# Gated attention with a ReGLU block on one core: raw scores for a second query tile in both halves of six heads, other tile counts per round, last stage reordered

## The chip, the core and the metric

The kernel runs on one NeuronCore of a Trainium2 chip. The core has a matrix engine (TensorE, PE in the profile; its weight loads, which overlap the matmuls, are PEld) and four others: VectorE (DVE), ScalarE (ACT), GpSimd (POOL) and SyncE (SP), which here only issues DMAs. Each engine works through its own list of instructions in order; semaphores join the lists. TensorE writes into eight PSUM banks of 128 x 512 floats, which are called bank 0 to bank 7 here. The metric is the device time of one execution in microseconds; lower is better.

## What is computed

```python
def _A_ref(x, wqkv, wo):          # S = 2048 tokens, D = 448, H = 16 heads of Dh = 28
    qkv = transpose((x @ wqkv).reshape(B, S, 3, H, Dh), 2, 0, 3, 1, 4)
    q, k, v = qkv[0], qkv[1], qkv[2]
    p = softmax(einsum("bhqd,bhkd->bhqk", q, k) * Dh ** -0.5)
    o = einsum("bhqk,bhkd->bhqd", p, v)
    return transpose(o, 0, 2, 1, 3).reshape(B, S, D) @ wo

def _B_ref(x, W_gate, W_up, W_down):                                    # F = 1792
    gate, up = x @ W_gate, x @ W_up
    return (gate * (gate > 0) * up) @ W_down

g = sigmoid((x * gate_w).sum(-1, keepdims=True))
return g * _A_ref(x, wqkv, wo) + (1 - g) * _B_ref(x, W_gate, W_up, W_down)
```

Everything is in float32. Matmuls run on operands that are split into a high and a low part, so each product is a sum of several matmuls.

## The kernel before, in words

**Stages.** First the projections: Q, K and V of all heads are computed and written to DRAM. Then 32 rounds, two for each head: round r belongs to head h = r // 2 and handles 8 of its 16 key tiles (128 keys each) against all 2048 queries, which are four query tiles j = 0 to 3 of 512. Last, a stage with the down projection (56 steps of 12 matmuls, four token tiles of 14 steps each), the output product of the attention, and the gated sum.

**A round.** Its matmuls stand in the order that a string of the table `ROUNDS` gives. Each letter is one instruction or a few: `s` a score matmul, whose tile ScalarE turns into exp (`scores`); `m` a score matmul whose maximum over the keys VectorE takes (`smax`), for a later head; `x` one of the matmuls of a gate/up tile (20 in a tile, in `gu_mm`); `r` a raw score matmul for the next round, copied out by ScalarE (`raw_scores`); `d` VectorE's running maximum over those copies (`raw_max`); `e` ScalarE's exponential of a raw tile of this round (`raw_exp`). A digit is the bank. Behind the string come the half-height last terms of the gate/up tiles, the rest of the exponentials, and 64 narrow matmuls of the weighted sum with V into bank 3 (`pv`).

**Two ways to the maximum.** The softmax needs the largest score of each query. For most query tiles it is found ahead of time, by `smax`: one matmul and one VectorE reduction for each 128 queries and 512 keys. For a raw tile no such pass is made: the scores of the round are copied out as they are, VectorE keeps a running maximum, and the end of the round before (`raw_top`) reduces it over the partitions: on VectorE two transposes, a reduction, four copies, a small reduction and a small transpose; then a DMA to DRAM (`mr_d`) and a DMA that broadcasts it back to all partitions. Next, GpSimd subtracts it from each raw tile (`raw_less`, 8 tiles for one query tile, 16 for two), and ScalarE takes the exponential. `raw_js(r)` says which query tiles are raw: j = 3 in every round from 2 on, and j = 2 too in the second (odd) round of the heads in `WIDE`. The odd round's sums are brought to the even round's maximum with a factor (`factors`, a GpSimd product behind the subtractions).

**What stands behind what.** At the end of a round VectorE's list has `raw_top` for the next round, then `spill_h` for the one or two gate/up tiles of the round (the product of gate and up, which frees banks 5 and 7 and goes to DRAM), then the copy or the sum that takes the weighted sum out of bank 3. `raw_top` writes its maxima over those that this round's subtractions read, so it waits for them. GpSimd's list has the subtractions, the factor product, the DMA of the spilled tiles, and in the early rounds the low halves of gate/up weights (`split_f`), then small products for the normalisation of the head before.

**The last stage** is a list `todo` of steps, run in order; a step `(down, i)` first issues the loads for step i + 4 (`fetch_d`: 128 rows of W_down and a tile of gate*up, from SyncE) and the splits for step i + 2 (`split_d`, ScalarE then VectorE). Between them stand the split of the output weight (`split_wo`), the row sums, their broadcast and the normalisation of head 15 (`row_sums`, `spread`, `normalise`), and for each token tile the load of the attention output (`fetch_o`), its split and four output products (`wout`).

## Time and profile before

| | us |
|---|---|
| median of 3 runs | 1220.13 (1219.09 to 1220.66) |
| the profiled execution | 1217.39 |
| its span, first to last instruction | 1215.6 |
| projections, up to the end of round 0's weighted sum | 168.5 |
| rounds 1 to 31 | 168.5 to 1025.6 |
| last stage | 1025.6 to 1215.6 |
| TensorE busy | 1205.0 |
| VectorE, ScalarE, GpSimd busy | 904.6, 815.7, 554.4 |

In a row of a group, after the names, stand the count, the busy time and the mean length in ns, then the idle time before it and what ended it. The busy time is the union of the group's own instructions; TensorE's overlap with those of other groups, so their busy times add up to more than the engine's. In a row in order of time the first two numbers are the start and the length in us. `PEclk` in the rows of a stretch is the granted clock, the third number from the end.

### The profile page before, as it was taken

Reading aid. Unit: us, or ns where it says so; the run is one execution under the profiler, and the core shown is the slowest. Engines: PE = TensorE matmul, PEld = TensorE weight load, DVE = VectorE, ACT = ScalarE, POOL = GpSimd, SP = SyncE. Lnnn points to the kernel's source line nnn. Section 1 sums busy time; section 2 is a strip of 40 time slices with the busy share of each in tenths; the row PEclk is TensorE's granted clock in tenths of the full one; section 3 lists DMA queues with packets and bytes.
Section 4 is the critical chain, followed back from the end, with each engine's and each line's share of the span. In section 5 each row is a group of like instructions: output and inputs, shape, how many; then the busy total and the mean of one; then the engine's idle time right before and its main releaser. Section 6 shows DMA issues by size and latency. Waiting matters only on the chain.

```text
span 1215.6 us, 18731 instructions
## 1 busy us (share of the span) xinstructions
PE 1205.0 (99%) x6399; PEld 866.3 (71%) x6399; DVE 904.6 (74%) x1606; ACT 815.7 (67%) x1615; POOL 554.4 (46%) x561
## 2 busy tenths in 40 slices
PE   9999999999999999999999999999999999899998
PEld 6888766666666666666666666656666756789997
DVE  6498777877887897888888889988888862453342
ACT  5311667788788777887888787888788886422121
POOL 4332325566553745474548446543847654300000
PEclk9999999999999999999999999999999999899999
DMA  8956745363645454445634343554353433653432
GB/s 298 341 212 245 252 167 188 111 205 103 213 151 176 136 166 122 130 123 185 193 119 156 108 127 108 166 187 137 109 171 90 146 96 101 221 184 113 139 105 81
DMA packets 68275, 193.99 MB, mean 160 GB/s; under 512 B 14850, under 2 KB 21602, under 8 KB 63754
## 3 DMA queue, kind: packets, MB, share of 16 engines
q1 hardware_dynamic: 55188, 148.02, 38.4%
q0 software_dynamic: 12560, 44.32, 10.2%
q8 instruction: 50, 0.82, 0.3%
q10 hardware_dynamic: 432, 0.46, 0.1%
q14 instruction: 45, 0.37, 0.1%
HBM read 132.09 MB, written 61.11 MB: 159 GB/s over the span
## 4 chain that ended last, share of the span: by engine, by line
PE 92%; ACT 3%; DMA 3%; DVE 1%; issue 0%; SPq 0%; POOL 0%; ACTq 0%; DVEq 0%
PE b L690 22%; PE b L728 19%; PE b L282 13%; PE b L309 13%; PE b L985 9%; PE b L503 6%; PE b L317 5%; PE b L521 3%; PE b L944 3%; ACT P L311 2%; DMA hr<-h_d 1%; DMA or<-o_d 1%; ACT P L321 1%; DMA wor<-wo_d 1%; DMA rb<-l_d 0%
## 5 line engine op out<-in xcount | busy, mean ns | idle before, releaser
L284 DVE TENSOR_REDUCE mx<-b 128x1 f32<-128x512 f32 x736 | 478.4, 686 | 50.6 <-PE b L282 45.0
L311 ACT ACTIVATE P<-b 128x512 f32<-128x512 f32 x728 | 402.8, 625 | 58.6 <-PE b L309 55.6
L690 PE MATMUL b<-X,wg 128*128 128x512 f32 (+1 forms) x1232 | 407.5, 400 | 0.3 <-POOL wg L187 0.3
L282 PE MATMUL b<-K,Q 128*128 128x512 f32 x736 | 272.5, 392 | 0.3 <-DVE mx L284 0.3
L309 PE MATMUL b<-Q,K 128*128 128x512 f32 x736 | 270.0, 392 | 0.0
L690 PEld LDWEIGHTS b<-X,wg 128*128 128x128 f32 (+1 forms) x1232 | 218.9, 188 | 67.5 <-issue 21.2
L728 PE MATMUL b<-P,v 128*32 128x512 f32 x1696 | 226.8, 594 | 0.0
L350 POOL TENSOR_TENSOR V<-V,P 128x512 f32<-128x512 f32 x168 | 211.0, 1296 | 24.2 <-DMA P<-mr_d 24.2
L712 POOL DMA_DIRECT2D h_d<-rl x56 | 31.3, 559 | 302.4 <-DVE rl L706 295.7
L350 POOL TENSOR_TENSOR P<-P,P 128x512 f32<-128x512 f32 x120 | 150.8, 1294 | 30.6 <-DMA P<-mr_d 15.4
L324 DVE TENSOR_TENSOR P<-b,P 128x512 f32<-128x512 f32 x231 | 156.4, 684 | 9.2 <-ACT V L321 3.8
L309 PEld LDWEIGHTS b<-Q,K 128*128 128x128 f32 x736 | 138.0, 188 | 33.5 <-ACT P L311 1.2
L282 PEld LDWEIGHTS b<-K,Q 128*128 128x128 f32 x736 | 138.0, 188 | 33.5 <-ACT P L311 1.3
L728 PEld LDWEIGHTS b<-P,v 128*32 128x32 f32 x1696 | 63.3, 110 | 121.5 <-issue 111.0
L985 PE MATMUL b<-WD,hh 128*128 128x448 f32 x672 | 142.0, 372 | 4.2 <-DVE WD L184 2.7
L985 PEld LDWEIGHTS b<-WD,hh 128*128 128x128 f32 x672 | 128.2, 191 | 16.7 <-DVE WD L184 3.1
L321 ACT ACTIVATE V<-b 128x512 f32<-128x512 f32 x160 | 94.7, 611 | 41.4 <-PE b L317 39.6
L728 PE MATMUL b<-V,v 128*32 128x512 f32 x352 | 113.8, 594 | 0.4 <-ACT V L354 0.4
L317 PE MATMUL b<-Q,K 128*128 128x512 f32 x288 | 111.2, 393 | 0.0
L178 ACT ACTIVATE hh<-hr 128x512 fp32r<-128x512 f32 x56 | 35.3, 631 | 110.8 <-PE b L985 109.4
L354 ACT ACTIVATE V<-V 128x512 f32<-128x512 f32 x168 | 96.6, 674 | 0.0
L184 DVE TENSOR_TENSOR hh<-hr,hh 128x512 fp32r<-128x512 f32 x56 | 38.6, 690 | 58.7 <-ACT hh L178 58.4
(103 smaller groups left out, 1080.1 us busy)
## 6 DMA issues: line engine op xcount, KB each, us to landing
wg<-wgs_d SPq DMA_DIRECT2D x42, 896.0 KB
K<-qk_d SPq DMA_DIRECT2D x64, 224.0 KB
Q<-qk_d SPq DMA_DIRECT2D x64, 224.0 KB
h_d<-rl POOLq DMA_DIRECT2D x56, 256.0 KB, 3.7
hr<-h_d SPq DMA_DIRECT2D x56, 256.0 KB
wgs_d<-wg SPq DMA_DIRECT2D x14, 896.0 KB
qk_d<-st POOLq DMA_DIRECT2D x21, 512.0 KB, 4.7
wgr<-wgu SPq DMA_DIRECT2D x13, 512.0 KB
```

What stands on the lines that cost most here:

```text
L282: nc.tensor.matmul(ps, Q[h][:, u * P:(u + 1) * P], K[h % 3][:, c * TB:(c + 1) * TB], start=True, stop=True)
L284: nc.vector.tensor_reduce(MX[h][:, at:at + 1], ps, axis=AX.X, op=OP.max)
L309: nc.tensor.matmul(ps, K[h % 3][:, kt * P:(kt + 1) * P], Q[h][:, j * TB:(j + 1) * TB], start=True, stop=True)
L311: nc.scalar.activation(prob(i, j), ps, AF.Exp, scale=SCALE)
L317: nc.tensor.matmul(ps, K[h % 3][:, kt * P:(kt + 1) * P], Q[h][:, j * TB:(j + 1) * TB], start=True, stop=True)
L321: nc.scalar.activation(own, ps, AF.Copy)
L324: nc.vector.tensor_tensor(run(3 - j), ps, run(3 - j) if i % 8 > 1 else prob(i - 1, j), op=OP.max)
L350: nc.gpsimd.tensor_tensor(own, own, top(3 - j), op=OP.subtract)
L354: nc.scalar.activation(own, own, AF.Exp, scale=SCALE)
L690: nc.tensor.matmul(ps, WS[i][rows, s, a], xf(i // NF, b)[rows], start=(n == 0), stop=(n == NT - 1))
L728: nc.tensor.matmul(po[32 * j:32 * j + 32], VH[h][:, i % NK], prob(i, j), start=(i == i0), stop=(i == i0 + ni - 1))
L985: nc.tensor.matmul(ACC[i // NF][t][:, :D], HH[i][:, a, t * P:(t + 1) * P], WD[:, f, b], start=(f == 0 and n == 0), stop=(f == NF - 1 and n ...
```

## The change

Three things are changed.

1. A new set `BOTH` = (4, 6, 8, 10, 12, 13), and head 2 joins `WIDE`. In the heads of `BOTH` both query tiles 2 and 3 are raw in both rounds; in head 2 in the second round. For a head of `BOTH`, `smax` covers 8 blocks of 128 queries instead of 12. In the even rounds of `BOTH` the raw tiles of j = 2 lie in the buffer `V`, in the odd ones in their own slots, so that those of two successive rounds don't meet.
2. The table `ROUNDS` is replaced. Gate/up tiles per round in the cycle of four rounds that heads 5 to 12 repeat were 1 (odd head, second half), 2, 2 (a `WIDE` head) and 2 (the next head's first half); the odd head now has 1 tile in its first half and 2 in its second. The rounds still do 55 of the 56. The next weights are asked for when a round's tiles are finished (`fin`) and no longer when they are begun.
3. In the last stage the load of the output weight stands behind the first four `fetch_d`, the reciprocal of head 15's row sums before the first down step, its normalisation before the eighth (was: the fifth), the splits of the output weight before steps 4 to 7 (was: 2 and 3), the first `fetch_o` before step 8 (was: 4) and from SyncE's queue (was: GpSimd's), its products before step 13, and head 15's last writes go to SyncE's queue.

**GpSimd, round 12** (head 6, first half; `os` is the weighted sum of a head, `V` and `P_...` are raw tiles, `P_1587` and `P_1539` the maxima). Before (the first three and the last of round 12's eight):

```order
L737 DMA ls_4297<-os_4078 128x1x16
L350 TENSOR_TENSOR P_1091<-P_1091,P_1587 128x512
L350 TENSOR_TENSOR P_1133<-P_1133,P_1587 128x512
L350 TENSOR_TENSOR P_1177<-P_1177,P_1587 128x512
L350 TENSOR_TENSOR P_1378<-P_1378,P_1587 128x512
L712 DMA h_d_4521<-rl_4499 128x512
L712 DMA h_d_4524<-rl_4501 128x512
L758 TENSOR_TENSOR os_4078<-os_4078,rb_4405 128x512
L187 TENSOR_TENSOR mh_4568<-mr_4567,mh_4568 12x128
L350 TENSOR_TENSOR V<-V,P_1587 128x512 x16
L369 TENSOR_TENSOR os_4564<-os_4564,fa_4590 64x512
```

Now (the first four and the last two of the 16 of round 12, and the first two of round 13's):

```order
L741 DMA ls_4312<-os_4036 128x1x16
L354 TENSOR_TENSOR P_1091<-P_1091,P_1539 128x512
L354 TENSOR_TENSOR V<-V,P_1539 128x512
L354 TENSOR_TENSOR P_1133<-P_1133,P_1539 128x512
L354 TENSOR_TENSOR V<-V,P_1539 128x512
L354 TENSOR_TENSOR P_1378<-P_1378,P_1539 128x512
L354 TENSOR_TENSOR V<-V,P_1539 128x512
L716 DMA h_d_4532<-rl_4507 128x512
L716 DMA h_d_4535<-rl_4509 128x512
L762 TENSOR_TENSOR os_4036<-os_4036,rb_4494 128x512
L189 TENSOR_TENSOR mh_4579<-mr_4578,mh_4579 8x128
L354 TENSOR_TENSOR V<-V,P_1539 128x512
```

Eight subtractions have become 16, and 16 more follow in round 13 as before.

**TensorE, start of round 14** (`b_69` to `b_76` are banks 0 to 7; L690/L694 gate/up, L282/L286 maxima, L309/L313 scores, L317/L321 raw scores). Before:

```order
L728 MATMUL b_72<-V,v_3874 32x512 x2
L690 MATMUL b_73<-X_166,wg_1242 128x512
L309 MATMUL b_70<-Q_177,K_174 128x512
L317 MATMUL b_75<-Q_177,K_174 128x512
L282 MATMUL b_76<-K_175,Q_178 128x512
L282 MATMUL b_71<-K_175,Q_178 128x512
L690 MATMUL b_73<-X_166,wg_1242 128x512
L309 MATMUL b_69<-Q_177,K_174 128x512
```

Now:

```order
L732 MATMUL b_72<-V,v_3886 32x512
L694 MATMUL b_73<-X_166,wg_1242 128x512
L321 MATMUL b_76<-Q_177,K_174 128x512
L286 MATMUL b_69<-K_175,Q_178 128x512
L321 MATMUL b_75<-Q_177,K_174 128x512
L694 MATMUL b_73<-X_166,wg_1242 128x512
L313 MATMUL b_71<-Q_177,K_174 128x512
```

Bank 7 (`b_76`), which `spill_h` of round 13 empties, is wanted by the second matmul of the round and no longer by the fourth.

**VectorE, last stage** (`WD` and `hh` are the splits for the down steps, `rs` the reciprocal, `os` head 15's weighted sum). Before:

```order
L184 TENSOR_TENSOR hh_9174<-hr_9127,hh_9174 128x512
L184 TENSOR_TENSOR WD<-wdr_9132,WD 128x448
L184 TENSOR_TENSOR hh_9183<-hr_9134,hh_9183 128x512
L745 RECIPROCAL rs_9198<-ls_9110 128x16
L184 TENSOR_TENSOR hh_9212<-hr_9138,hh_9212 128x512
L184 TENSOR_TENSOR hh_9237<-hr_9179,hh_9237 128x512
L184 TENSOR_TENSOR hh_9262<-hr_9208,hh_9262 128x512
L758 TENSOR_TENSOR os_8952<-os_8952,rb_9201 128x512
```

Now:

```order
L186 TENSOR_TENSOR hh_9219<-hr_9172,hh_9219 128x512
L749 RECIPROCAL rs_9222<-ls_9155 128x16
L186 TENSOR_TENSOR hh_9236<-hr_9176,hh_9236 128x512
L186 TENSOR_TENSOR hh_9257<-hr_9180,hh_9257 128x512
L186 TENSOR_TENSOR hh_9278<-hr_9232,hh_9278 128x512
L186 TENSOR_TENSOR hh_9299<-hr_9253,hh_9299 128x512
L186 TENSOR_TENSOR hh_9322<-hr_9274,hh_9322 128x512
L186 TENSOR_TENSOR hh_9345<-hr_9295,hh_9345 128x512
L186 TENSOR_TENSOR hh_9368<-hr_9318,hh_9368 128x512
L762 TENSOR_TENSOR os_8997<-os_8997,rb_9225 128x512
```

Between the reciprocal and the product that uses it stood three splits of `hh`, and now seven (the splits of `WD` in between are left out here).

The diff, cut to its core:

```diff
 ROUNDS = [
...
-    ("xs0xm1r7m6m2r3dxs0s1xs6m7xs2xm3s1m0s7xm6r3s2m1xs0xds6m7s1s2m0r3xm6s1xs2s0dm7m6xs1m3r2r7xds0xs6dxes1xxm3m2xr0"
-     "s7s6xedm3r1m2xs7s0ds6"),
-    ("xr6s2xm7xr1m6r3m0dxr2s1xs6xr7dxm0s1xs2s3dxxm0s6m1s2m3s7xs6m0m1s2m7s3s6r0xr2xm3xs6r7dxxs3xdxs0m6s1xxr3r2xs1xs"
-     "0dxddxr7m3s1xds0xm2s3r1xm7xr2m0dxs3xxexdexm0r3xxm1xdxer2xxr1dxs0d"),
...
+    ("xxs2s6m0s1r3m7xr2xm6m1r7s3xdm0r2xm6s1s3xr7xr0ddm1xs6s3xs2xxs6xds3m7m2r0xr1dxs3xds6r2m7xds3exs0xm6xm7r1r2m3xr"
+     "0xxedr7xxxexddr1xxr2dm0m3exxxxxdeexdexr0xexm1xs2xd"),
+    ("xxs0r2m7xm3r1s6m0ds7xs2m3xm6xr0xs1s2s7ds3m6xxxm0m1xs6xm7xs2m3s0m1em7xm6s3es2xm1xxr7m0xm6em2xxer3ds0xxxem1xdx"
+     "s0m2xxm7xr0xm3dem1xer2xxxr3exxdxs1dm0xxxm2xm1"),
...
-WIDE = (4, 6, 8, 10, 12, 13)
+WIDE = (2, 4, 6, 8, 10, 12, 13)
+
+BOTH = (4, 6, 8, 10, 12, 13)
...
-        return [] if r < 2 else [3, 2] if r % 2 and r // 2 in WIDE else [3]
+        return [] if r < 2 else [3, 2] if r // 2 in (WIDE if r % 2 else BOTH) else [3]
...
-            if r % 2 == 0:
+            if j == 3 and r % 2 == 0:
                 return slot(k)[:, 3]
+            if j == 2 and r % 2 and r // 2 in BOTH:
+                return slot(k)[:, 2]
...
-        return NK if h == 0 else NK - 4
+        return NK if h == 0 else NK - 8 if h in BOTH else NK - 4
...
-            side(h).dma_start(o_d[DH * h:DH * (h + 1), j * TB:(j + 1) * TB], o[32 * j:32 * j + DH])
+            nc.sync.dma_start(o_d[DH * h:DH * (h + 1), j * TB:(j + 1) * TB], o[32 * j:32 * j + DH])
...
-        if asked < NB * NF and parts == 2 * NF and (asked == NF or nxt >= asked - 2):
+        if asked < NB * NF and parts == 2 * NF and (asked == NF or fin >= asked - 2):
...
-        queue = nc.sync if tb else nc.gpsimd
-        queue.dma_start(r[:, 0:3], o_d[0:3 * P, t].rearrange("(c p) t -> p c t", p=P))
+        nc.sync.dma_start(r[:, 0:3], o_d[0:3 * P, t].rearrange("(c p) t -> p c t", p=P))
...
-    todo = [(gate_up, i) for i in range(done, NB * NF)]
+    todo = [(split_d, 0)] + [(gate_up, i) for i in range(done, NB * NF)] + [(split_d, 1), (row_sums, H - 1), (spread, H - 1)]
...
-    before(1, (row_sums, H - 1), (spread, H - 1))
-    before(4, (normalise, H - 1))
+    before(7, (normalise, H - 1))
     for c in range(4):
-        before(2 + c // 2, (split_wo, c))
-    for tb, load, split, at in ((0, 4, (9, 10), (12, 12, 13, 13)), (1, 8, (12, 14), (17, 18, 19, 20)), (2, 21, (23, 25), (28,) * 4),
+        before(4 + c, (split_wo, c))
+    for tb, load, split, at in ((0, 8, (12, 12), (13,) * 4), (1, 13, (15, 16), (17, 18, 19, 20)), (2, 21, (23, 25), (28,) * 4),
...
     for i in range(4):
         fetch_d(i)
-        if i == 1:
-            load_wo()
+    load_wo()
```

More of the change, by code (lines that the diff above doesn't have):

```diff
@@ L287, in smax @@
             mx = MX.pop(h)
-            for u0, u1, b, at in ((0, 8, 4, 0), (8, 12, 2, 32)) if h in WIDE else ((0, n, 4, 0),):
+            for u0, u1, b, at in ((0, 8, 4, 0), (8, 12, 2, 32)) if h in WIDE and n > 8 else ((0, n, 4, 0),):
                 nc.vector.tensor_reduce(M[h][:, u0:u1], mx[:, at:at + b * (u1 - u0)].rearrange("p (a b) -> p a b", b=b),
@@ L1036, in gated_mix_kernel @@
         fetch_d(i)
-        if i == 1:
-            load_wo()
-    start = todo.index((down, 0)) - 1
-    for n, (f, *a) in enumerate(todo):
-        if n in (start, start + 1):
-            split_d(n - start)
+    load_wo()
+    for f, *a in todo:
         if f is down:
```

105 lines of the change are left out of this document (53 added, 52 removed).

## The prediction

> **What bounds the kernel now.** I read the page's busy times first, then its groups, then TensorE in order of time, and then each engine round by round.
>
> ```profile
> span 1215.6 us, 18731 instructions
> PE 1205.0 (99%) x6399; PEld 866.3 (71%) x6399; DVE 904.6 (74%) x1606; ACT 815.7 (67%) x1615; POOL 554.4 (46%) x561
> L284 DVE TENSOR_REDUCE mx<-b 128x1 f32<-128x512 f32 x736 | 478.4, 686 | 50.6 <-PE b L282 45.0
> L282 PE MATMUL b<-K,Q 128*128 128x512 f32 x736 | 272.5, 392 | 0.3 <-DVE mx L284 0.3
> L350 POOL TENSOR_TENSOR V<-V,P 128x512 f32<-128x512 f32 x168 | 211.0, 1296 | 24.2 <-DMA P<-mr_d 24.2
> L324 DVE TENSOR_TENSOR P<-b,P 128x512 f32<-128x512 f32 x231 | 156.4, 684 | 9.2 <-ACT V L321 3.8 <-ACT P L321 2.8
> ```
>
> TensorE is busy for 99% of the span, so a matmul that disappears is time, at a price still to be found: 392 ns is the length of one matmul, but they overlap. In order of time, 29 matmuls of 512 columns start from the first of these rows up to the second.
>
> ```profile
> 299.81 0.39 PE L309 MATMUL b<-Q,K 128*128 128x512 f32 x1
> 306.43 0.39 PE L309 MATMUL b<-Q,K 128*128 128x512 f32 x1
> 306.75 0.73 PE L690 MATMUL b<-X,wg 64*128 64x512 f32 x4
> 307.41 0.63 PE L728 MATMUL b<-P,v 128*32 128x512 f32 x3
> 314.41 0.50 PE L690 MATMUL b<-X,wg 128*128 128x512 f32 x1
> ```
>
> (306.43 - 299.81) / 29 = 0.228 us is what one costs. The half-height last terms and the weighted sum, which end a round, take 314.41 - 306.75 = 7.7 us (the sum alone 7.0), whatever the change does.
>
> Now rounds 10 to 13 (heads 5 and 6), one row each.
>
> ```profile
> 428.50:459.20 30.70, 30.70 (x170) 20.80 (x170) 26.55 (x52) 21.90 (x42) 13.83 (x14) 1.00 0.54 170
> 459.20:483.20 24.00, 24.00 (x140) 15.89 (x138) 19.54 (x36) 21.16 (x44) 12.39 (x11) 1.00 0.39 128
> 483.20:513.80 30.60, 30.60 (x169) 20.23 (x168) 26.60 (x48) 25.80 (x50) 12.30 (x12) 1.00 0.42 121
> 513.80:541.60 27.80, 27.80 (x157) 18.50 (x157) 24.22 (x42) 22.74 (x45) 23.18 (x20) 1.00 0.38 114
> ```
>
> Columns: length, then busy time of PE, weight loads, DVE, ACT, POOL. TensorE is never idle; DVE comes to 87%, ACT to 84% of its length. Only in round 13, with 16 raw tiles to lower, has GpSimd much to do.
>
> **The matmuls removed.** Head 2 gets maxima over half the keys for four query tiles (48 to 40), the heads of `BOTH` none at all for them (40 to 32): 56 fewer, 56 x 0.228 = **-12.8 us**. Raw scores take the place of scores that were computed anyway, so TensorE gains nothing else. The new counts of gate/up tiles only move tiles between rounds: 55 are done by round 31 as before, and the half-height last terms pair up as before.
>
> **What the 56 extra raw tiles ask of the others.** 56 maxima leave DVE; 49 running maxima (L324, as long as a maximum) and seven longer `raw_top` come: about nothing. ACT gets 56 more copies, GpSimd 56 more subtractions. Round 12 of the change has 16 scores, 16 raw copies, 16 exponentials and 2 relus: 50 on ACT, as many as in round 12 now (25.80 us). The round has 88 matmuls at full height, against 98 in round 12 and 87 in round 13 now, so it lasts 30.6 - 2.3 = 28.3 or 27.8 + 0.2 = 28.0 us (I take 28.0): ACT at 92%. I price that at nothing; what hides it is that banks 0 to 3, 6 and 7 take a lag of some evictions. If they don't, it is the ScalarE case below.
>
> **The chain of subtractions.** This is the step that decides. These are round 12's end and round 13 now: DVE, the SyncE queue, GpSimd.
>
> ```profile
> 506.94 1.29 DVE L330 STREAM_TRANSPOSE P<-P 128x512 f32<-128x512 f32 x2
> 511.23 1.29 DVE L706 TENSOR_TENSOR rl<-b,rl 128x512 f32<-128x512 f32 x2
> 513.88 0.69 DVE L732 COPY os<-b 128x512 f32<-128x512 f32 x1 [1.36 <-PE b L728]
> 536.54 0.71 DVE L330 STREAM_TRANSPOSE P<-P 128x512 f32<-128x512 f32 x1 [1.84 <-POOL V L350]
> 540.16 1.26 DVE L706 TENSOR_TENSOR rl<-b,rl 128x512 f32<-128x512 f32 x2
> ...
> 511.12 0.30 SPq L343 DMA_DIRECT2D mr_d<-row_b  x1
> 512.52 0.34 SPq L346 DMA_DIRECT2D P<-mr_d  x1
> 540.25 0.31 SPq L343 DMA_DIRECT2D mr_d<-row_a  x1
> ...
> 517.68 20.08 POOL L350 TENSOR_TENSOR V<-V,P 128x512 f32<-128x512 f32 x16 [2.51 <-DMA P<-mr_d]
> ```
>
> The 16 subtractions begin 517.68 - 513.80 = 3.9 us into the round and take 20.1. The next round's `raw_top` overwrites the maxima that they read, so its transposes wait (1.84 us at 536.54). Now that costs nothing: the spills still end at 540.16 + 1.26 = 541.4, 0.2 us before the round does, and only 8 subtractions follow. In the change 16 follow 16, in rounds 8-9, 12-13, 16-17, 20-21, and four times running in 24 to 27.
>
> From the end of 16 subtractions to the start of the next 16: second transpose to the write of the maxima 511.12 - 507.58 (half of the pair's 1.29 after 506.94) = 3.5; to the broadcast 1.4; to the first subtraction 517.68 - 512.52 = 5.2. Together 10.1, so the chain has a period of 20.1 + 10.1 = 30.2 us, and the rounds are shorter: 28.0 us, and the odd one of a pair, with 89 matmuls, 28.25.
>
> What is late is DVE. Behind `raw_top` stand the two spills, which free bank 7 (1.4 us after the write of the maxima, 511.12 to 512.52), then the copy that frees bank 3 (0.7).
> - Round 8 from 0: subtractions 3.9 to 24.0; bank 7 free at 24.0 + 3.5 + 1.4 = 28.9, bank 3 at 29.6. Round 9 wants bank 7 with its fifth matmul, 28.0 + 4 x 0.228 = 28.9, and bank 3 two matmuls later, 29.4: about 0.3 us lost.
> - Round 9, to 28.0 + 0.3 + 28.25 = 56.55: subtractions 34.1 to 54.2, the 15th done at 52.9. One transpose now, but 540.25 - 536.54 = 3.7 to the write, 1.2 to the spills' end: bank 7 at 57.8. Round 10 wants it with its second matmul, 56.8: 1.0 lost. The last exponential (54.2 + 0.7) comes before its weighted sum (56.55 - 0.9), so nothing there.
>
> So 1.3 a pair, 4 x 1.3 = 5.2 us. For heads 12 and 13 the same steps, with the lateness carried along: round 25 loses 0.2 at bank 7; its `raw_top` of two tiles beside GpSimd's factor product ends 3.5 + 0.8 behind 54.2, bank 3 is free at 60.6, and round 26 (from 56.45) wants it with its seventh matmul at 57.8: 2.8; round 27 waits 2.2 at banks 7 and 3, round 28 0.6. Sum 5.8. In round 5 the subtractions start later,
>
> ```profile
> 284.43 6.04 POOL L187 TENSOR_TENSOR wg<-wgr,wg 128x384 fp32r<-128x384 f32 x8
> 292.11 10.08 POOL L350 TENSOR_TENSOR V<-V,P 128x512 f32<-128x512 f32 x8
> ```
>
> 6.0 us into the round (from 286.1), behind weight splits; 16 of them end at 26.1 of about 27 us: 0.6 lost at the last key tile, 1.6 at bank 7 in round 6, 1.0 for its weights, whose splits queue behind the spills' DMAs. 3.2. In sum **+14.2 us**. Bounds: 0, if the subtractions start 1.5 us earlier than in round 13, and 22, if each of the 15 waits is 0.5 us longer.
>
> **The last stage.** Down projection after the rounds, then what ACT and DVE waited for, the queue, and the clock.
>
> ```profile
> 1030.75 5.03 PE L985 MATMUL b<-WD,hh 128*128 128x448 f32 x24
> 1037.13 10.52 PE L985 MATMUL b<-WD,hh 128*128 128x448 f32 x49 [1.34 <-ACT hh L178]
> 1050.34 17.80 PE L985 MATMUL b<-WD,hh 128*128 128x448 f32 x71 [2.69 <-DVE WD L184]
> 1067.97 4.71 PE L944 MATMUL b<-WO,on 128*128 128x448 f32 x22
> 1134.40 34.21 PE L985 MATMUL b<-WD,hh 128*128 128x448 f32 x168
> ...
> 1035.75 0.58 ACT L178 ACTIVATE WD<-wdr 128x448 fp32r<-128x448 f32 x1 [3.85 <-DMA wdr<-wd]
> 1037.72 0.24 DVE L745 RECIPROCAL rs<-ls 128x16 f32<-128x16 f32 x1
> 1048.93 0.82 DVE L758 TENSOR_TENSOR os<-os,rb 128x512 f32<-128x512 f32 x1 [5.28 <-DMA rb<-l_d]
> ...
> 1027.57 0.45 SPq L904 DMA_DIRECT2D wor<-wo_d  x1
> 1029.31 0.64 SPq L968 DMA_DIRECT2D wdr<-wd  x1
> ...
> 1037.00:1050.00 13.00, 10.47 (x49) 9.06 (x49) 5.55 (x10) 8.73 (x18) 7.02 (x9) 0.99 0.78 246
> 1050.20:1057.00 6.80, 6.66 (x18) 5.71 (x19) 4.72 (x9) 1.09 (x2) 3.75 (x7) 0.54 0.82 263
> ```
>
> 34.21 / 168 = 0.204 us a matmul; the 144 from 1030.75 to 1067.97 should take 29.3 and took 37.2: 7.9 lost. Two causes. The third load of W_down is queued behind the whole output weight; the change puts that behind the fourth. And DVE stands 5.28 us at the normalisation of head 15, with splits queued behind it; its factors land 1048.93 - 1037.72 = 11.2 us behind the reciprocal. The change has the reciprocal ahead of the third split and the multiplication before the eighth down step, 7 x 12 x 0.204 = 17 us after the first. After that gap the clock stood at 0.54 for 6.8 us, which is part of the 7.9. I leave 1.5 us for what is late next: the o_d writes and the first `fetch_o`, now on SyncE, stand ahead of loads for down step 12. **-6.4 us**, between -3 (the output weight's transfer delays a later step as it now delays the third) and -7.9 (nothing left).
>
> **Sum.** -12.8 + 14.2 - 6.4 = -5.0. The profiled execution took 1217.4 us (span 1215.6 and 1.8 around it), so 1212.4; the median of the runs is 2.7 above it: **1215 us**.
>
> **Rivals.**
> - *The chain costs nothing.* For it: the 1.84 us in which DVE waits for subtractions leave no mark on TensorE in round 13 now. Against it: there the spills end 0.2 us before the round, and 0.9 us behind it in round 8 by the sum above. It decides if the subtractions start below 2.5 us into an even round. 1220.1 - 12.8 - 6.4 = 1201, with some small waits 1202.
> - *The clock drops in the new waits.* For it: the 2.69 us before 1050.34 were followed by 0.54; against it, the 1.34 before 1037.13 were not. The waits of 2.8 and 2.2 us in rounds 26 and 27 lie between. Half of 6.8 us, twice: 1215 + 6.8 = 1222. The Trainium skill (TensorE: Matmul & The Clock Gate, Part 1) has the gate close after an idle window of about 3.4 us; by that rule neither wait closes it and 1215 stands, but in this trace 2.69 us sufficed.
> - *ScalarE becomes the bound* (the slower side). In the loop of an even round of `BOTH` it has 16 + 16 + 8 = 40 evictions in 28.0 - 7.7 = 20.3 us. At 25.80 / 50 = 0.516 each they take 20.6; what goes beyond, TensorE waits for banks. At 0.56 it is 22.4 - 20.3 = 2.1 us in each of six rounds: 1215 + 13 = 1228. From 0.54 on the kernel is slower than before. Against it: round 12 now has 24 + 16 + 3 = 43 in 30.6 - 7.7 = 22.9 us, 1.9 a us against 2.0, and no idle TensorE.
>
> **How the numbers follow.** Forecast 0.42, no chain cost 0.30, clock 0.12, ScalarE 0.16. A measurement of this kernel tells 0.2% from no change: 1217.7 and 1222.6. The forecast's own range is 1209 to 1221; nine tenths of it count as faster. Faster 0.38 + 0.30 = 0.68; the same 0.04 + 0.11 = 0.15; slower 0.17. The range reaches from the second case, 1201, to 1224, short of the full price of ScalarE.
>
> **What would show it.** The maxima's group with 680 instead of 736; subtractions of round 9 starting 6 us into it rather than 3.9; matmuls at the start of rounds 9, 10, 26 and 27 released by `spill_h` or by the copy in `pv`; no idle over 1 us and no clock below 1.00 between the rounds' end and the first output product. I am wrong if rounds 8 to 10 come to no more than 28.0 + 28.25 + 24.0 us, or if ACT is what ends the waits inside their loops.

## The result: half a per cent slower

The changed kernel takes 1224.88 us (median of 9 runs, 1222.67 to 1230.52) against 1219.39 us for the kernel before on the same chip: a ratio of 1.0053, 95% interval 1.0035 to 1.0071. The forecast was 1215 us, faster. The profiled execution took 1224.52 us. First the page's head, the groups and the shares of the chain that ended last, of the kernel after:

```profile
span 1222.7 us, 18800 instructions
PE 1198.0 (98%) x6343; PEld 851.0 (70%) x6343; DVE 909.1 (74%) x1594; ACT 841.0 (69%) x1671; POOL 622.1 (51%) x610
PE 71%; POOL 11%; DMA 8%; DVE 4%; ACT 2%; issue 2%; SPq 1%; DVEq 0%; POOLq 0%; ACTq 0%
L288 DVE TENSOR_REDUCE mx<-b 128x1 f32<-128x512 f32 x680 | 441.4, 685 | 50.2 <-PE b L286 46.0
```

The 56 matmuls are gone (6343 instead of 6399, 680 maxima instead of 736), and TensorE's busy time fell by 7.0 us. But 11% of the chain is now GpSimd's and 12% transfers and VectorE (before, 92% of it was TensorE). The waits of the kernel after, who for whom, total, times, longest:

```profile
DVE P L334 <- POOL V L354: 24.4, 13, 5.3
DVE P L334 <- POOL P L354: 15.4, 7, 4.2
PE b L286 <- DVE rl L710: 5.6, 3, 2.2
```

VectorE's transposes in `raw_top` stand 40 us behind the subtractions, and matmuls of the maxima behind `spill_h` (L710), where they had waited 0.3 us for VectorE in all. Where: stretches of rounds 8, 9, 10 and of 12 and 14 of the kernel after (length, then busy time of PE, weight loads, DVE, ACT, POOL; the granted clock is third from the end).

```profile
369.50:397.76 28.26, 28.26 (x160) 18.34 (x156) 21.88 (x36) 25.41 (x50) 20.82 (x17) 1.00 0.59 191
397.76:430.26 32.50, 30.32 (x162) 19.71 (x158) 28.50 (x55) 22.86 (x45) 24.35 (x22) 0.95 0.34 107
430.26:454.76 24.50, 23.97 (x140) 15.08 (x136) 20.29 (x41) 20.67 (x41) 13.57 (x13) 1.00 0.70 219
485.80:514.00 28.20, 28.20 (x160) 18.40 (x156) 24.59 (x46) 25.23 (x50) 20.81 (x17) 1.00 0.56 182
542.41:569.10 26.69, 24.23 (x138) 15.10 (x136) 22.00 (x47) 20.63 (x41) 13.74 (x13) 1.00 0.61 201
```

Rounds 8 and 12, the even rounds with 16 subtractions, are about as long as forecast (28.0), with ScalarE at 90% of their length. The loss is at the starts of rounds 9 and 14, and round 9 ran at a mean clock of 0.95.

To add it up I take, from the trace, by how much the starts of neighbouring matmuls are further apart than 0.228 us (0.204 in the down steps), and call the sum of a stretch its waits; a round without any has 0.6 to 0.9. The weighted sums' own delays are hardly in it.

| part | forecast | waits before | after | difference |
|---|---|---|---|---|
| rounds 8-10 | +1.3 | 2.5 | 7.2 | +4.7 |
| rounds 12-14 | +1.3 | 2.4 | 5.1 | +2.8 |
| rounds 16-18 | +1.3 | 2.4 | 6.4 | +4.0 |
| rounds 20-22 | +1.3 | 2.1 | 4.1 | +2.0 |
| rounds 24-28 | +5.8 | 3.4 | 11.7 | +8.3 |
| rounds 5, 6 | +3.2 | 1.5 | 5.0 | +3.5 |
| together | +14.2 | | | +25.3 |
| last stage | -6.4 | 8.7 | 5.0 | -3.6 |

-12.8 + 25.3 - 3.6 = +8.9, where the two profiled executions differ by 7.1; the rest are the weighted sums, which took 1.8 us less in all (round 7's took 8.15 us before and 6.91 after, while round 5's grew by 1.5). So each term has its sign, and in the forecast the chain of subtractions is 11 us too small.

### The profile page after: what moved, and what is told of

It is laid out like the page before. It is cut to its first block, busy times and chain, and to the rows that moved or that the text cites. A ratio compares the mean times of both kernels' runs of the same rounds, so it can differ in the third digit from the quotient of the medians.

```text
span 1222.7 us, 18800 instructions
## 1 busy us (share of the span) xinstructions
PE 1198.0 (98%) x6343; PEld 851.0 (70%) x6343; DVE 909.1 (74%) x1594; ACT 841.0 (69%) x1671; POOL 622.1 (51%) x610
## 4 chain that ended last, share of the span: by engine, by line
PE 71%; POOL 11%; DMA 8%; DVE 4%; ACT 2%; issue 2%; SPq 1%; DVEq 0%; POOLq 0%; ACTq 0%
PE b L694 15%; PE b L732 12%; PE b L286 10%; PE b L313 10%; PE b L989 9%; POOL V L354 6%; PE b L507 6%; POOL P L354 4%; PE b L321 4%; PE b L525 3%; PE b L948 3%; DMA P<-mr_d 2%; DMA mr_d<-row_a 1%; DMA wdr<-wd 1%; ACT P L315 1%
## 5 line engine op out<-in xcount | busy, mean ns | idle before, releaser
L288 DVE TENSOR_REDUCE mx<-b 128x1 f32<-128x512 f32 x680 | 441.4, 685 | 50.2 <-PE b L286 46.0
L315 ACT ACTIVATE P<-b 128x512 f32<-128x512 f32 x672 | 374.0, 627 | 71.3 <-PE b L313 69.3
L694 PE MATMUL b<-X,wg 128*128 128x512 f32 (+1 forms) x1232 | 401.0, 401 | 1.3 <-POOL wg L189 1.0
L694 PEld LDWEIGHTS b<-X,wg 128*128 128x128 f32 (+1 forms) x1232 | 218.5, 188 | 71.6 <-issue 22.7
L286 PE MATMUL b<-K,Q 128*128 128x512 f32 x680 | 254.1, 395 | 10.1 <-DVE rl L710 5.6
L313 PE MATMUL b<-Q,K 128*128 128x512 f32 x680 | 245.6, 394 | 1.8 <-DVE rl L710 1.8
L354 POOL TENSOR_TENSOR V<-V,P 128x512 f32<-128x512 f32 x176 | 225.3, 1297 | 24.4 <-DMA P<-mr_d 24.4
L354 POOL TENSOR_TENSOR P<-P,P 128x512 f32<-128x512 f32 x168 | 215.2, 1296 | 33.9 <-DMA P<-mr_d 25.2
L328 DVE TENSOR_TENSOR P<-b,P 128x512 f32<-128x512 f32 x279 | 185.0, 682 | 13.9 <-ACT P L325 6.3
L286 PEld LDWEIGHTS b<-K,Q 128*128 128x128 f32 x680 | 127.6, 189 | 44.6 <-DVE rl L710 6.9
L732 PE MATMUL b<-V,v 128*32 128x512 f32 x368 | 156.0, 594 | 0.4 <-ACT V L358 0.4
L313 PEld LDWEIGHTS b<-Q,K 128*128 128x128 f32 x680 | 127.6, 188 | 35.8 <-DVE rl L710 2.6
L321 PE MATMUL b<-Q,K 128*128 128x512 f32 x344 | 131.6, 394 | 3.9 <-DVE rl L710 2.6
L358 ACT ACTIVATE V<-V 128x512 f32<-128x512 f32 x176 | 111.8, 673 | 3.7 <-POOL V L354 3.5
L325 ACT ACTIVATE P<-b 128x512 f32<-128x512 f32 x160 | 98.7, 624 | 16.3 <-PE b L321 15.0
```

The source lines that it names most:

```text
L286: nc.tensor.matmul(ps, Q[h][:, u * P:(u + 1) * P], K[h % 3][:, c * TB:(c + 1) * TB], start=True, stop=True)
L288: nc.vector.tensor_reduce(MX[h][:, at:at + 1], ps, axis=AX.X, op=OP.max)
L313: nc.tensor.matmul(ps, K[h % 3][:, kt * P:(kt + 1) * P], Q[h][:, j * TB:(j + 1) * TB], start=True, stop=True)
L315: nc.scalar.activation(prob(i, j), ps, AF.Exp, scale=SCALE)
L321: nc.tensor.matmul(ps, K[h % 3][:, kt * P:(kt + 1) * P], Q[h][:, j * TB:(j + 1) * TB], start=True, stop=True)
L325: nc.scalar.activation(own, ps, AF.Copy)
```

## The experiments

A time is the median; a ratio is to the kernel before on the same chip. That kernel's own median lay between 1218.33 and 1220.47 us on the chips used, so times of different experiments can be compared to some 2 us. "Waits" are those of the sum above, rounds 1 to 31 (22.8 before, 47.7 after).

### The last stage alone: e2_tail

The kernel before with the change's last stage (everything from `fetch_o` on) and `normalise` writing from SyncE's queue; rounds and `ROUNDS` as before.

> The kernel before with the change's last stage alone. Reading of the two traces: the last stage takes 186.4 us in place of 190.0, so 1216 us. By the prediction's working 1213. If the last stage hurts without the rest, 1220 or more.

1212.76 us, ratio 0.9938 (0.9917 to 0.9960). By itself the last stage gains 0.6%, so it is the rounds that lose: 1224.88 against 1212.76 with the same last stage. Its down steps, in order of time:

```profile
1030.41 30.36 PE L984 MATMUL b<-WD,hh 128*128 128x448 f32 x144
1062.37 3.02 PE L984 MATMUL b<-WD,hh 128*128 128x448 f32 x12 [1.60 <-ACT hh L178]
```

The 144 matmuls that took 37.2 us before take 30.4 in one piece. What is late next is a split before the first output products: 1.60 us here. The changed kernel has the same wait:

```profile
1051.79 20.41 PE L989 MATMUL b<-WD,hh 128*128 128x448 f32 x96 [0.17 <-ACT hh L180]
1073.86 4.33 PE L989 MATMUL b<-WD,hh 128*128 128x448 f32 x12 [1.66 <-ACT hh L180]
...
1064.25 0.38 SPq L925 DMA_DIRECT2D or<-o_d  x1
1072.41 0.58 ACT L180 ACTIVATE WD<-wdr 128x448 fp32r<-128x448 f32 x1 [5.05 <-DMA wdr<-wd]
```

It is a load of W_down that stands behind `fetch_o` in the queue, as the forecast had it.

### Are GpSimd's subtractions the cause: e3_longer

```diff
             raw_less(i, j)
+            if len(exps) == 16 and k == 0:
+                own = prob(i, j)
+                for op in (OP.add, OP.subtract):
+                    nc.gpsimd.tensor_tensor(own, own, top(3 - j), op=op)
```

> The change, with two more GpSimd operations (the maxima are added back and subtracted again on the first tile) in each of the 13 rounds with 16 subtractions: 2.5 us more on GpSimd a round, none on the other engines. Theory: the chain's period grows by 2.5 us wherever 16 follow 16 and both waits behind it do: 5 us for each of the four pairs, 10 for rounds 24 to 28, 2.5 for round 5, about 30 us in all, 1250 to 1258. Rival (load of VectorE and ScalarE): GpSimd has slack of 4 us a round, so no change, 1225.

1262.13 us in its one run, 37 above the changed kernel and more than expected. Rounds 1 to 31 took 34.3 us of it (902.2 against 867.9), for 13 rounds with 2.6 us more of GpSimd's work each (33.8). In this order of the work, GpSimd's time in these rounds is TensorE's time.

### Free VectorE from them: e1_order

The subtractions and exponentials in the order of the query tiles (all of tile 3, then all of tile 2), and `raw_top` transposes both tiles through the maxima of tile 3, which are then free after eight subtractions.

```diff
-        for a in range(n):
-            nc.vector.transpose(top(a), run(a))
+        for a in range(n):
+            nc.vector.transpose(top(0), run(a))
+            nc.vector.tensor_reduce(small[:, 16 * a:16 * a + 16], top(0)..., axis=AX.X, op=OP.max)
...
+        exps.sort(key=lambda e: -e[1])
         for i, j in exps:
             raw_less(i, j)
```

> The change, with the link taken out that makes VectorE wait for GpSimd at the end of a round: the subtractions run query tile by query tile (all eight of j = 3, then all of j = 2; the exponentials in the same order), and raw_top transposes and reduces one query tile after the other through the one area that the first eight subtractions free. Only the broadcast then waits for the 16th subtraction. Theory (the chain of subtractions costs the 25 us that the rounds lost): the wait of the transposes for GpSimd goes from 40 us to below 5, rounds 9, 10, 14, 17, 18, 22, 25 to 27 come within 1 us of 28.2 and 24.0 us, and the kernel takes 1205 to 1210 us. Rival (VectorE and ScalarE are simply too full in the rounds of the set): nothing is taken from their work, so 1224 to 1227 us.

1221.78 us, ratio 1.0019 (0.9998 to 1.0039), waits 43.7. VectorE no longer waits at the transposes, and yet the gain is 3 us, where 15 to 20 were expected. Round 13 of e1_order, GpSimd and VectorE in order of time:

```profile
531.83 6.29 POOL L354 TENSOR_TENSOR P<-P,P 128x512 f32<-128x512 f32 x5
533.75 0.70 DVE L335 STREAM_TRANSPOSE P<-P 128x512 f32<-128x512 f32 x1
534.48 0.69 DVE L336 TENSOR_REDUCE P<-P 128x16 f32<-128x512 f32 x1
535.20 4.47 DVE L339 COPY P<-P 32x16 f32<-32x16 f32 x4
538.19 1.28 POOL L373 TENSOR_TENSOR os<-os,fa 64x512 f32<-64x512 f32 x1
```

The transpose and the reduction ran at their usual length beside the subtractions. Then four copies of 32x16 took 4.47 us: the first until the subtractions ended, the third until the factor product had ended. The write of the row followed at 540.24. The line of the copies, after and in e1_order (shortest, median, longest in ns):

```profile
L339 DVE COPY P<-P x120: 161/169/1142, 193.0 to 1009.8; 32x16 f32<-32x16 f32 x68, 32x32 f32<-32x32 f32 x52
```

```profile
L339 DVE COPY P<-P x120: 161/169/5111, 192.8 to 1011.4; 32x16 f32<-32x16 f32 x68, 32x32 f32<-32x32 f32 x52
```

In e1_order 15 of the 120 took 33.5 us together, the other 105 took 0.17 each.

### The copies as reductions: e5_order_reduce and e7_reduce

```diff
-            nc.vector.tensor_copy(four[:, a, :16 * n], best[32 * a:32 * a + 32])
+            nc.vector.tensor_reduce(four[:, a, :16 * n], best[32 * a:32 * a + 32].rearrange("p (c o) -> p c o", o=1), axis=AX.X, op=OP.max)
```

> The order of e1_order, with the four copies of 32x16 ahead of each row of maxima written as reductions over one element. In e1_order 15 of these 120 copies took 33.5 us together while GpSimd was subtracting (the longest 5.11 us, ending with the last subtraction), and the other 105 took 0.17 us each. Theory: VectorE's copies cannot run beside GpSimd's subtractions, and that took back what the new order gave; a reduction ran its usual 0.69 us beside them, so the time falls from 1221.8 to 1205-1212 us and no such reduction takes over 0.4 us. Rival: the loss in e1_order is SyncE's queue that stands at the broadcast of the maxima with the loads of queries and weights behind it; then it stays at 1218-1224.

> The changed kernel with only the copies written as reductions. There six of the 120 copies took 1.1 us rather than 0.17, each the first one behind the last subtraction of a round. Theory: this lies in the chain ahead of the next subtractions, 1 us each in six rounds, so 1217-1222 us. Rival: the wait of VectorE for the subtractions is what counts and the copies are hidden: 1223-1226.

e5_order_reduce: 1212.95 us, ratio 0.9953 (0.9940 to 0.9967), 8.8 us under e1_order and 1 us outside what was expected; waits 33.0. e7_reduce (the changed kernel with this edit alone): 1220.57 us, ratio 1.0009 (0.9991 to 1.0026), 4.3 under the changed kernel. The line of e5_order_reduce, with the same count and shapes:

```profile
L339 DVE TENSOR_REDUCE P<-P x120: 156/161/178, 192.8 to 999.7; 32x16 f32<-32x16 f32 x68, 32x32 f32<-32x32 f32 x52
```

None is over 0.18 us. The same data at the same place, so it was the kind of instruction. The Trainium skill (SBUF — State Buffer, Who interferes with whom) says that VectorE and GpSimd share a pair of ports, that a copy can take it and one of the two engines then blocks for whole instructions, and that a reduction never does on this chip; this trace agrees, with 0.17 against up to 5.11 us.

### The 2 MB in front of three broadcasts: e4_queue, e8_no_x, e10_x_out

In rounds 7, 15 and 23 the next 512 tokens are loaded. Here is the end of round 7 of the kernel after, SyncE's queue and then GpSimd:

```profile
358.61 4.50 SPq L698 DMA_DIRECT2D X<-x_d  x8
363.17 3.14 SPq L258 DMA_DIRECT2D K<-qk_d  x4
366.82 0.32 SPq L347 DMA_DIRECT2D mr_d<-row_a  x1
372.15 0.34 SPq L350 DMA_DIRECT2D P<-mr_d  x1
376.07 1.29 POOL L354 TENSOR_TENSOR P<-P,P 128x512 f32<-128x512 f32 x1 [4.52 <-DMA P<-mr_d]
```

From the write of the row to its broadcast 5.3 us (1.4 in round 12 of the kernel before), so the subtractions of round 8 begin 376.07 - 369.50 = 6.6 us in; in rounds 16 and 24 it is 6.2 and 6.4. e4_queue put these two DMAs into ScalarE's queue for the three rounds:

```diff
-        nc.sync.dma_start(mr_d[r][:16 * n], row[:16 * n])
+        queue = nc.scalar if r in (8, 16, 24) else nc.sync
+        queue.dma_start(mr_d[r][:16 * n], row[:16 * n])
...
-        nc.sync.dma_start(top(0, n), ...)
+        queue.dma_start(top(0, n), ...)
```

> The change, with the two DMAs of raw_top for rounds 8, 16 and 24 issued from ScalarE's queue in place of SyncE's. In rounds 7, 15 and 23 SyncE's queue loads the next 512 tokens of x, and the broadcast is issued 5 us behind the write of the maxima there, 1.3 to 2.5 elsewhere. If that lateness is what makes the pairs 8-9, 16-17 and rounds 24 to 27 dearer than pairs 12-13 and 20-21: subtractions of rounds 8, 16 and 24 start at 3 to 4 us rather than 6.2 to 6.6, and 5 to 7 us are gained, 1218 to 1220. If the DMA rings themselves are full, or ScalarE is held up by waiting for VectorE, 1224 or more.

1237.25 us, ratio 1.0134 (1.0107 to 1.0161): worse. In e4_queue:

```profile
368.18 0.34 ACTq L348 DMA_DIRECT2D mr_d<-row_a  x1
374.41 0.35 ACTq L351 DMA_DIRECT2D P<-mr_d  x1
374.87 1.58 ACT L315 ACTIVATE P<-b 128x512 f32<-128x512 f32 x3 [7.18 <-DMA mr_d<-row_a]
```

The write took 6.2 us from another queue too, so it isn't SyncE's queue that holds it; the run without the loads, below, shows that the bytes do. And ScalarE, which can't issue the broadcast until the write has arrived, evicted nothing for 7.18 us. e8_no_x and e10_x_out were to leave these loads out:

```diff
-        if i % NF == NF - 1 and s and i < NB * NF - 1 and (n == NT - 1 or ...):
+        if not i and (n == NT - 1 or ...):              # e8_no_x
+        if i > NB * NF and (n == NT - 1 or ...):        # e10_x_out
```

> The changed kernel without the loads of the next 512 tokens in rounds 7, 15 and 23 (2 MB each; the gate and up products of all tokens then use the first 512). Theory: the row of maxima written at the end of these rounds takes 4.8-5.3 us to arrive because it stands behind these 2 MB, so the subtractions of rounds 8, 16 and 24 start at 2.5-3 us rather than 6.2-6.6, and rounds 8-10, 16-18 and 24-27 lose 8-12 us of their waits: 1211-1217 us. Rival: VectorE's wait for the last subtractions alone makes these rounds long: 1221-1225.

> The changed kernel with the loads of the next 512 tokens left out altogether (e8_no_x had put them into the first gate and up products, where they cost 35 us). The gate and up products of all tokens use the first 512. From the rounds of e8_no_x, where rounds 8-10, 16-18 and 24-27 had 19.3 us of waits rather than 24.5: 1217-1221 us. If the late broadcast were the whole surplus over the forecast, 1211-1214; if nothing of it, 1223-1226.

Without these loads the gate and up products of all tokens use the first 512. e8_no_x moved the loads into the first gate and up products instead of dropping them and took 1256.62 us (35 us were lost by the end of round 0), not the 1211 to 1217 expected; only its later rounds say something. e10_x_out, without the loads: 1219.50 us, ratio 0.9990 (0.9976 to 1.0005), 5.4 below the changed kernel, as expected the second time. Write and broadcast there:

```profile
366.83 0.32 SPq L347 DMA_DIRECT2D mr_d<-row_a  x1
368.18 0.34 SPq L350 DMA_DIRECT2D P<-mr_d  x1
```

1.35 us apart. Its waits are 41.3, so these loads, and the late broadcasts behind them, are some 6 of the 25 us; rounds 12-14 and 20-22, which have no such load, keep theirs (5.0 and 4.0).

### What else stands in the queue: e6_early, e9_send_last, e12_keys_last, e13_keys_last_2

All four are e5_order_reduce with SyncE's queue in another order. In e6_early:

```diff
-        if r % 2 and h + 3 < H:
-            load_k(h + 3)
         if r % 2 == 0:
             next_w()
-        if raws(r + 1) and r:
-            raw_top(r + 1)
+        second = raw_top(r + 1) if raws(r + 1) and r else []     # sends tile 3 only
+        if r % 2 and h + 3 < H:
+            load_k(h + 3)
...
         for _ in range(2):
             next_w()
+        for send in second:                                      # tile 2
+            send(1)
```

> As e5_order_reduce, and in SyncE's queue the write of the maxima stands ahead of the next keys, the broadcast of tile 3 right behind it, and that of tile 2, which has to wait for the last subtraction, behind the loads of queries and weights. Theory of the copies and of the queue together: the subtractions of rounds 9, 13, 17, 21, 25-27 start 0-4 us into their rounds rather than 5.7-8.9, and the time is 1197-1206 us. If the queue costs nothing it comes out like e5_order_reduce; if the 16 subtractions of 20 us are themselves too long for a round, 1215 or more.

1223.52 us, ratio 1.0031 (1.0010 to 1.0053); 10.6 slower than e5_order_reduce, which it was to beat. The subtractions did start sooner in rounds 10 and 14 (2.1 us in), but in rounds 9, 13, 17 and 21, where 0 to 4 us was expected, they started at 5.1 to 5.8. The loads of keys, queries and weights came later, and matmuls of the maxima waited 10 to 12 us into rounds 10, 18, 22 and 24 (1.7 to 3.3 us from start to start), in the last three for queries. e9_send_last went the other way: where the next round is 8, 16 or 24, the broadcast is issued at that last place, behind the loads of queries and weights.

> As e5_order_reduce, and only in the three rounds that load the next 512 tokens the broadcast of the maxima goes to SyncE's queue behind the loads of the next queries and weights. In e5_order_reduce rounds 8 and 24 still have 4.8 and 4.4 us of waits, mostly of gate and up products (3.9 and 2.4), and the broadcast ahead of them was issued 5.1 and 3.0 us into these rounds, with the weights behind it in the queue. Theory: the weights stand behind the broadcast, which stands behind 2 MB; the two rounds fall to about 1.5 us of waits each and the time from 1213 to 1205-1210 us. Rival: the weights are late because of the 2 MB themselves, whatever the order: 1212-1215.

1227.87 us, ratio 1.0062 (1.0043 to 1.0082). Rounds 8, 16 and 24 have 7.3, 7.7 and 6.8 us of waits, the others 0.6 to 1.7. In e9_send_last, round 8:

```profile
371.28 0.32 SPq L351 DMA_DIRECT2D P<-mr_d  x1
381.58 7.51 POOL L359 TENSOR_TENSOR P<-P,P 128x512 f32<-128x512 f32 x6 [11.93 <-DMA P<-mr_d]
```

The broadcast took 10.3 us behind 4 loads of queries and 2 of weights. Theory and rival both failed: in these runs neither the weights nor the broadcast could be last without a loss. So the keys, wanted last, went to the end:

```diff
-        if r % 2 and h + 3 < H:
+        if r % 2 and h + 3 < H and r % 8 != 7:
             load_k(h + 3)
...
+        if r % 8 == 7 and h + 3 < H:
+            load_k(h + 3)
```

> As e5_order_reduce, and in the three rounds that load the next 512 tokens the load of the keys of three heads on (0.9 MB) goes behind the loads of queries and weights instead of ahead of the row of maxima. In e9_send_last everything but these three rounds had come down to its least (29 rounds with 0.6 to 1.7 us of waits each), and these three had 21.8 us because the broadcast took 10 us behind queries and weights. Theory: what counts there is how many bytes are ahead of the row and of the broadcast in the transfer engines; with the keys behind them the broadcast is issued 1-1.5 us into rounds 8, 16 and 24 rather than 3-5, the subtractions start at 4-5 us, and the time is 1204-1210 us. If the keys are late instead, the score products of the maxima wait for them 10 us into the rounds and it stays at 1211-1215 us.

1219.45 us (12 runs, 1214.29 to 1222.03), ratio 0.9991 (0.9977 to 1.0005): neither of the two times expected, though both mechanisms came. Rounds 8 and 16 fell to 0.84 us of waits each. Round 24 rose to 10.0, nearly all one wait for keys (profiled execution of e12_keys_last, the shortest of the 12; SyncE's queue and TensorE):

```profile
820.00 4.35 SPq L258 DMA_DIRECT2D K<-qk_d  x4
832.88 0.77 PE L286 MATMUL b<-K,Q 128*128 128x512 f32 x1 [7.67 <-DMA K<-qk_d]
```

e13_keys_last_2 does this in rounds 7 and 15 alone.

> As e12_keys_last, but round 23 keeps its keys ahead of the row of maxima. In e12_keys_last rounds 8 and 16 came down to 0.84 us of waits each (4.8 and 1.4 in e5_order_reduce) and round 24 rose to 10.0, of which 7.7 us is one wait for keys. Theory: what the new rounds lost is made of waits only, and with rounds 8 and 16 at their least and round 24 at 4.4 as in e5_order_reduce, the rounds have 27-29 us of waits in all rather than 47.8 in the changed kernel: 1205-1210 us, under the 1212.8 of the old rounds with the new last stage, so that the 56 matmuls saved pay. Rival: the new rounds can't be brought under the old ones, 1212-1216 us.

1211.93 us, ratio 0.9934 (0.9914 to 0.9953). The waits fell to 28.4, as expected; the time didn't reach 1205 to 1210. What my sum of waits doesn't hold had grown: the weighted sums of the even rounds took 7.7 to 7.9 us instead of 6.91.

### The order of the exponentials: e14_exps and e15_exps_even

The strings hold only 8 of a round's 16 exponentials; by query tiles, all of tile 2 come after the round, and the weighted sum waits for them.

```diff
         for i, j in exps:
             raw_less(i, j)
+        if r % 2 == 0:
+            exps.sort(key=lambda e: e[0] + 1.5 * (e[1] == 2))
```

e14_exps is this without the condition.

> As e13_keys_last_2 (1211.9 us), with the exponentials put back nearly into the order of the key blocks, while the subtractions stay in the order of the query tiles. In e13_keys_last_2 the products with v take 7.7-7.9 us rather than 6.91 in the ten rounds whose following tiles are not all ready (rounds 8, 12, 16, 20, 24-26 among them), because only eight of the sixteen exponentials stand in the round and in the new order the eight of query tile 2 all come after it. Theory: this takes back 0.75 us in each, 6-7 us in all, and hid what the new rounds save: 1204-1208 us. Rival: the subtractions of query tile 2 come too late for exponentials in the old order, and ScalarE stands in its queue inside the rounds instead: 1211-1216 us.

> As e14_exps, with the order of the exponentials put back in even rounds alone. In e14_exps rounds 8, 12, 16 and 20 fell to 28.2 us each (29.0 in e13_keys_last_2) and their products with v to 6.91 us, while in the odd rounds 9, 13, 17, 21 and 27, where exponentials stand early in the round, ScalarE waited 6 us for a subtraction and TensorE 5-6 us behind it, with its clock down afterwards. Theory: the even rounds keep their gain of 0.8 us in each of six, the odd ones come back to 28.3: 1206-1209 us against the 1211.9 of e13_keys_last_2. Rival: what the even rounds gain is lost to a later start elsewhere: 1211-1214 us.

e14_exps: 1247.42 us, ratio 1.0217 (1.0191 to 1.0244). Rounds 8, 12, 16 and 20 had their 28.2 us, and rounds 9, 13, 17, 21 and 27 took 35.9 to 36.7. Round 9 of e14_exps, ScalarE and TensorE:

```profile
413.82 0.63 ACT L358 ACTIVATE P<-P 128x512 f32<-128x512 f32 x1 [5.60 <-POOL P L354]
415.99 0.80 PE L313 MATMUL b<-Q,K 128*128 128x512 f32 x1 [5.27 <-ACT P L315]
```

There an exponential early in the string had to wait for its subtraction, and all of ScalarE's evictions stood behind it. e15_exps_even: **1207.51 us** (1204.72 to 1209.23), ratio 0.9904 (0.9885 to 0.9923), the fastest kernel of this study, below both kernels compared and below e2_tail. Its rounds 8, 9 and 10 (to be held against 28.26, 32.50 and 24.50):

```profile
367.36:395.63 28.27, 28.27 (x160) 18.40 (x156) 25.24 (x47) 25.28 (x50) 22.07 (x20) 1.00 0.72 217
395.63:423.99 28.36, 28.36 (x162) 18.92 (x158) 24.08 (x44) 23.00 (x45) 23.41 (x21) 1.00 0.41 124
423.99:447.81 23.82, 23.82 (x140) 14.99 (x136) 19.83 (x40) 20.52 (x41) 13.15 (x12) 1.00 0.62 211
```

Twenty us of subtractions in each of two successive rounds fit, then: TensorE never idles in rounds 8 to 10. The rounds came down by 18 us (1 to 31: 867.9 after, 849.7 here). What is left is mainly round 24, whose keys still stand ahead of the row: 32.3 us, with a wait of 1.98 us for queries.

### The same mends in the old rounds: e11_before_mended

e2_tail with the edits of e9_send_last.

> The kernel before with the new last stage (e2_tail, 1212.8 us) and the three edits of e9_send_last. It does the 56 matmuls more, 12.8 us. If the second set of raw queries pays once its waits are gone, this kernel is slower than e9_send_last, by 3-9 us: 1209-1213 us against 1205-1210. If the new rounds still lose what they save, the two are within 2 us of each other or this one is faster.

1219.29 us, ratio 0.9992 (0.9979 to 1.0005), slower than e2_tail by 6.5: the old rounds had nothing for these edits to free, and got the longer weighted sums (7.87 us in odd rounds) and a round 8 whose subtractions start 11.7 us in. That it is slower than e9_send_last, as one of its cases had it, did not happen, because e9_send_last failed. The edits of e15_exps_even were not run in the old rounds.

## Why the prediction was wrong

- **The matmuls removed, -12.8.** Right. 6343 are left, and in e15_exps_even rounds 1 to 31 take 7.5 us less than before (849.7 against 857.2) with 6.3 us more of waits and weighted sums 1.1 us shorter.
- **The 56 extra raw tiles at nothing.** Right. Round 12 took 28.20 us where I had 28.0, ScalarE at 25.23 / 28.20 = 89%, and the rival *ScalarE becomes the bound* did not come: inside the rounds no matmul waited over 0.4 us for an eviction by ScalarE.
- **The chain of subtractions, +14.2.** The mechanism was right (e3_longer), the size was not: +25.3, beyond the bound of 22. What the step followed came out in sum: the waits for banks 7 and 3 at the starts of rounds are 11.6 us in rounds 9 to 27, where I had 11.0, and those of rounds 5 and 6 are 3.5 against 3.2. They lie in other places, though. The step that begins "Round 8 from 0: subtractions 3.9 to 24.0" took the start that round 13 had for every even round. In rounds 8, 16 and 24 it is 6.2 to 6.6, behind 2 MB, so round 9 lost 2.35 us (0.3 forecast) and round 17 1.7, and nothing rounds 13 and 21. This stood in the trace of before, where round 8's broadcast followed the write by 6.5 us and landed at 377.62, so that its subtractions began 8.0 us in (the round starts at 369.8); they were eight and cost nothing:

```profile
377.76 2.54 POOL L350 TENSOR_TENSOR P<-P,P 128x512 f32<-128x512 f32 x2 [6.03 <-ACT P L311]
```

- **Where the step stopped too soon.** It followed the late VectorE to the two banks, and no further. From the end of round 12 into round 14 of the kernel after:

```profile
513.13 0.31 SPq L347 DMA_DIRECT2D mr_d<-row_b  x1
515.63 0.34 SPq L350 DMA_DIRECT2D P<-mr_d  x1
520.74 1.29 POOL L354 TENSOR_TENSOR V<-V,P 128x512 f32<-128x512 f32 x1 [3.65 <-DMA P<-mr_d]
544.49 0.50 PE L321 MATMUL b<-Q,K 128*128 128x512 f32 x1 [1.51 <-DVE rl L710]
544.59 0.35 SPq L350 DMA_DIRECT2D P<-mr_d  x1
544.99 3.09 SPq L264 DMA_DIRECT2D Q<-qk_d  x4
554.45 0.47 PE L286 MATMUL b<-K,Q 128*128 128x512 f32 x1 [0.95 <-DMA wg<-wgs_d]
```

  Round 13's broadcast follows the write by 2.5 us, not 1.4, and its subtractions begin 6.7 us in, not 5.8; round 14's second matmul is 1.8 us late, where I had 1.0. Then comes a second wait that the sum doesn't have, 12 us into the round. Its row names a load of weights, but the matmul reads keys and queries, and by the landings in the trace the last piece of the query loads came at 554.10, the first of those weights only at 554.30 and the last at 556.21. So it is the queries, queued behind the late broadcast, that hold TensorE. Rounds 10, 18, 22 and 24 have such a wait at the same place, whatever their rows name: the last queries landed 9.8, 10.6, 10.8 and 10.4 us in, 0.1 to 0.4 us ahead of the matmul. In the kernel before the queries of these five rounds landed 0.3 to 2.6 us sooner, and no matmul waited there. The five waits are 0.7 + 1.1 + 0.85 + 0.95 + 1.4 = 5.0 us.
- **The rival *the clock drops in the new waits*.** I gave it as a case apart; it came on top. The starts of rounds 27 and 17, then TensorE's busy time and clock in steps of 3.41 us around them:

```profile
920.04 0.50 PE L286 MATMUL b<-K,Q 128*128 128x512 f32 x1 [1.86 <-DVE rl L710]
631.50 0.50 PE L286 MATMUL b<-K,Q 128*128 128x512 f32 x1 [1.54 <-DVE rl L710]
```

```profile
918.18:921.59 3.41, 1.55 (x7) 1.11 (x7) 3.34 (x8) 1.08 (x3) 1.85 (x3) 1.00 0.22 31
921.59:925.00 3.41, 3.41 (x10) 2.64 (x9) 2.73 (x5) 2.11 (x5) 0.96 (x2) 0.50 1.00 285
628.02:631.43 3.41, 1.95 (x13) 0.69 (x5) 3.20 (x12) 1.66 (x4) 0.28 (x1) 1.00 0.21 80
631.43:634.84 3.41, 3.34 (x14) 2.59 (x15) 3.41 (x7) 1.97 (x5) 2.52 (x4) 1.00 0.64 207
```

  After 1.86 us the clock fell, after 1.54 it didn't; round 9's wait (2.19 us) did the same as round 27's. In both, seven matmuls then stand 0.43 us apart: 7 x 0.2 = 1.4 us, 2.8 together, where the rival had 3.4 each. Each drop is to exactly one half and lasts 3.41 us; the 6.8 us from which the rival took its price were two such steps in a row. The drops begin at 402.76, 921.59 and, in the last stage, 1075.19, which are 152 and 45 times 3.413 us apart, so they lie on a grid. In the step of that grid ahead of each, TensorE was idle for 1.91, 1.86 and 1.71 us; the longest idle of a step without a drop behind it was 1.51 us, in round 14. So it is not one wait that counts in these traces but the idle time of a step, about half of it. Against the rule of the Trainium skill (TensorE: Matmul & The Clock Gate, Part 1), an idle window of about 3.4 us, half of one was enough here.

  5.0 + 2.8 = 7.8 of the 11.1 us that were missing; 0.6 and 0.3 are the first waits' own, and the other 2.4 lie in many small ones. The late starts behind 2 MB (5.4 us by e10_x_out) are among the causes of all of these and not to be added.
- **The last stage, -6.4.** Alone, -6.5 (1212.76 - 1219.27, e2_tail). In the changed kernel the sum of its waits fell by 3.6 only, though it runs the same steps. In the profiles of the other kernels with this last stage these waits are 2.1 to 7.9 us, so a single profile doesn't tell the two apart. A drop of the clock goes with it: the ten profiles that have one in this stage take 186.5 to 189.7 us for it, the six without one 183.1 to 187.9. Why the waits differ I didn't test.
- **What would show it.** Of the signs named, the count of maxima, the releasers (`spill_h` at rounds 9 and 27, the copy in `pv` at round 26) and the time of rounds 8 to 10 (85.3 us, not 80.25) came. The subtractions of round 9 started 8.9 us in, not 6, and between the rounds and the first output product there was an idle of 1.66 us and then a clock of one half, both of which I had excluded.

## What to carry to other kernels

A start time that is read in one place of a repeating pattern has to be read in each place where it will matter, above all where another load falls due; work that is late without cost today shows there already. Follow a late engine through everything that its queue issues afterwards, not only to the first buffer that it frees, and price a wait on TensorE with its clock, by the idle time that gathers within one step of 3.41 us rather than by the wait alone. When an engine is to run ahead beside another, look at the length of each of its instructions there: a copy that stretches from 0.17 to 5 us is the wait in another dress, and a different instruction for the same data can remove it.

## What was unexpected of the hardware

- Small copies on VectorE took 0.17 us alone and 0.9 to 5.1 us beside GpSimd's operations, over several of them in a row; transposes, reductions and maxima that read PSUM kept their length beside them.
- TensorE's clock fell to one half for steps of 3.41 us on a fixed grid. In the 14 traces that have such a drop before the end, a step at full clock with less than 1.64 us of idle was never followed by one, and a step with more than 1.79 us always was. An idle of 5.27 us in e14_exps brought two steps in a row.
- A write of 4 KB took 5.3 us behind 2.9 MB of loads issued in the 8 us ahead of it (1.35 us without 2 MB of them), from another engine's queue 6.2, and a broadcast of 0.5 MB behind queries and weights took 10.3 us.
